# Query product and last group inside TensorE's loop, loads issued from a loop, a transpose in place of three spreads, last values behind w3 and w4

## The chip, the core and the metric

The kernel runs on one core of one Trainium2 chip. The core has five engines that run at the same time and meet through semaphores: TensorE (PE, matrix products), VectorE (DVE), ScalarE (ACT), GpSimd (POOL) and SyncE (SP, which here only issues transfers). Transfers between the chip's main memory (HBM) and the core's own memory (SBUF, 128 partitions) are carried out by 16 DMA engines. The metric is the device time of one execution in microseconds (us), shorter being better. Beside it stands the span, from the first to the last instruction of the one execution that was profiled.

## What is computed

Two blocks run on the same four rows of `x` (batch 4, one token each, width 512), and their results are added:

```python
xn = layernorm(x)
q = (xn @ wq).reshape(4, 1, 32, 128)             # 32 heads of 128
scores = einsum(q, k_cache) * 128 ** -0.5        # k_cache (4, 32, 4096, 128)
o = einsum(softmax(scores), v_cache)             # v_cache (4, 32, 4096, 128)
A = o.reshape(4, 1, 4096) @ wo                   # wo (4096, 512)
x1 = xn                                          # see below
B = x1 + gelu(layernorm(x1) @ w3) @ w4           # w3 (512, 1792), w4 (1792, 512)
out = x + A + B
```

The second block shifts its hidden rows by one or two tokens before `w2`. With one token per row the shift leaves only zeros, so neither kernel loads `w1` or `w2`. Everything is float32. The two caches are 268 MB each, so nearly all that the kernel does is to read 128 pairs (batch, head) of 2 MB of keys and 2 MB of values, once each.

## The kernel before

**Groups.** The 128 pairs (batch, head) are cut into 32 groups of four. A group's keys are 8.39 MB: each of the 128 partitions gets 64 KB, which is 128 cache rows of one head, and each head has 32 partitions. The values are laid out in the same way. Three slots of 8.39 MB in SBUF take the loads in turn: S1 and S0 take the keys of even and odd groups, S2 takes the values.

**One group.** DVE multiplies the keys in place with the query, spread over the rows (two instructions, L330 and L332, one for each half), sums each row over the 128 elements (L335), which gives the scores, and takes the maximum of each head's partitions (L337 to L340). ACT turns the scores into weights `pw` with their row sums `rs` (L238). TensorE contracts weights and values in 32 products (the helper `contract`), four of which share the array, each in 32 output rows. ACT copies the result out of PSUM (L244), and four products with the selector `sel` and one with `ones` turn it into four columns of outputs and sums (`outputs` of TensorE, L246 on ACT), which go to `OS`.

**The order of the work** is written out by hand. The work of each engine is one block (`@block.sync`, `.gpsimd`, `.tensor`, `.scalar`, `.vector`), and the loops over groups are hardware loops (`Fori`) on TensorE, ACT and DVE. SP's 75 loads are unrolled. SP issues them in one queue, and each waits until its slot is free: `k_free` comes from DVE after L335 of that group, `v_free` from TensorE after `contract`. `take` waits for a semaphore and counts it down again.

**The start.** SP issues `wq` in two halves and the keys of group 0 in two halves (L128, L123). TensorE multiplies `wq` outside its loop (32 products), ACT copies and scales two results (L228), DVE transposes them and copies them to `Q` (L316, L317). Only then, on `d_T`, does SP issue the keys of group 1, since their slot S0 holds the scratch data of the start.

**The end.** The values of group 31 go to S1 once the keys of group 30 are used (L141). `w3` and `w4` go to S2 once the values of group 30 are used (L143, L144). `wo` goes to S0 in six pieces once the keys of group 31 are used (L147, L148). After the loop TensorE spreads the outputs of batches 0 to 2 over the operand `X` of the last product (`spread`, with `lt`, which DVE builds in `normalised`), contracts the last values (`VL`), multiplies `w3`, builds the outputs of the last group, spreads batch 3, and multiplies `w4`. DVE and ACT work out gelu in between (L356 to L363, L263, L268). The last part stands in a critical section of its own (from L365 on): TensorE multiplies `wo` piece by piece as the pieces land. Rows 0 to 23 of each partition's 32 go as products of 512 columns into `y`, which ACT copies to `os` (L384) and TensorE adds to `total` by way of `sel`. The other eight rows go straight into `total`, each in four products of 128 columns (L377). DVE and ACT copy `total` to `res` (L386, L388), and SP and ACT each write one half of the output.

Of the kernel before, what the change touches and what calls it, by code (L numbers as in the profile page):

```python
# [7 lines left out]
F32 = mybir.dt.float32  # L8
# [5 lines left out]
P = 128  # L14
# [6 lines left out]
def decode_block(ctx: ExitStack, tc: tile.TileContext, x, k, v, wq, wo, w3, w4, out):  # L21
# [26 lines left out]
    X = sbuf("X", [P, WC, B])  # L48
# [3 lines left out]
    mask = sbuf("mask", [P, 4])  # L52
# [7 lines left out]
    ot = sbuf("ot", [P, JB, HG])  # L60
    rec = sbuf("rec", [P, JB, HG])
    lt = sbuf("lt", [P, H, 4])

    pv, oz, total, y, pa, pb = (nc.alloc_psum_tensor(f"ps{i}", [P, 512], F32) for i in range(6))
# [7 lines left out]
    PIECES = ((0, 8), (8, 16), (16, 24), (24, 28), (28, 31), (31, 32))  # L72
    CUT = 24
    s_x, s_v, s_vl, s_kh, s_h = (sem(n) for n in ("sx", "sv", "svl", "skh", "sh"))
    s_wq = [sem(f"swq{n}") for n in range(2)]
    s_k = [sem(f"sk{n}") for n in range(2)]
    s_wo = s_k + [s_v, s_x, s_kh, s_h]
    d_self, g_a, c_done, d_T, k_free, v_free = (sem(n) for n in ("dself", "ga", "cd", "dT", "kf", "vf"))
# [3 lines left out]
    vf = v.rearrange("b h s d -> (b h s d)")  # L82
# [9 lines left out]
    q_sb = S0[:, 4 * D:6 * D].rearrange("p (n f) -> p n f", n=2)  # L92
    qT = S0[:, 6 * D:8 * D]
    xp = S0[:, 8 * D:8 * D + 2 * P].rearrange("p (e c i) -> p e c i", e=2, c=NC)
    xnT = S0[:, 9 * D:9 * D + P].rearrange("p (c m) -> p c m", c=NC)
    wq_sb = S2[:, :].rearrange("p (c n) -> p c n", c=NC)
    w3_sb = S2[:, :NC * F].rearrange("p (c f) -> p c f", c=NC)
    w34 = NC * F + NF * D
    w4_sb = S2[:, NC * F:w34].rearrange("p (m n) -> p m n", m=NF)
    hs, gu, gt, gT = (S2[:, w34 + n * FT:w34 + (n + 1) * FT] for n in range(4))  # L100
    V3 = S2[:, :].rearrange("p (c d) -> p c d", c=C)
    VL = S1[:, :].rearrange("p (c d) -> p c d", c=C)
# [10 lines left out]

    with tc.tile_critical(no_gpsimd_drain=True), nc.Block(no_gpsimd_drain=True) as block:

        @block.sync
        def _(e):
            def load_k(g):
                e.dma_start(KS[g % 2][:, :], group(kf, g)).then_inc(s_k[g % 2], 16)

            def load_k_half(g, n, s):
                r = slice(n * ROW // 2, (n + 1) * ROW // 2)
                e.dma_start(KS[g % 2][:, r], group(kf, g)[:, r]).then_inc(s, 16)  # L123

            wq_r = wq.rearrange("(p c) n -> p c n", p=P)
            for n in range(2):
                c = slice(n * NC // 2, (n + 1) * NC // 2)
                e.dma_start(wq_sb[:, c, :], wq_r[:, c, :]).then_inc(s_wq[n], 16)  # L128
# [12 lines left out]
            e.dma_start(S1[:, :], group(vf, NG - 1)).then_inc(s_vl, 16)  # L141
            take(e, v_free)
            e.dma_start(w3_sb, w3.rearrange("(p c) f -> p c f", p=P)).then_inc(s_wq[0], 16)  # L143
            e.dma_start(w4_sb, w4.rearrange("(p m) n -> p m n", p=P)).then_inc(s_wq[1], 16)  # L144
            take(e, k_free)
            wo_r = wo.rearrange("(p c) n -> p c n", p=P)
            for n, (c0, c1) in enumerate(PIECES):  # L147
                e.dma_start(wo_sb[:, c0:c1, :], wo_r[:, c0:c1, :]).then_inc(s_wo[n], 16)  # L148

        @block.gpsimd  # L150
        def _(e):
            e.memset(xs, 0.0).then_inc(g_a, 1)
            e.memset(ident[:, :], 0.0).then_inc(c_done, 1)
            e.memset(rs[:, :], 0.0)
            e.memset(pw[:, :, :], 0.0).then_inc(g_a, 1)
# [3 lines left out]
            take(e, s_kh, 16)  # L159
            e.wait_ge(c_done, 2).then_inc(s_h, NG)  # L160

        @block.tensor
        def _(e):
            def contract(V):
                for g in range(G4):
                    t = g % 4
                    i = mm(e, pv[32 * t:32 * t + 32, :], pw[:, g, :], V[:, 4 * g:4 * g + 4, :], g < 4, g >= G4 - 4)
                return i

            def outputs(done):  # L170
                i = mm(e, oz[:, HG:2 * HG], ones[:, :], rs[:, :], True, True)
                if done is not None:
                    i.then_inc(done, 1)
# [4 lines left out]

            def spread(b):
                take(e, d_p)  # L180
                mm(e, pa[:, 32 * b:32 * b + 32], lt[:, :, :], sel[:, :], True, True).then_inc(p_a, 1)

            e.wait_ge(d_T, 1)
            for c in range(NC):
                if c % (NC // 2) == 0:
                    take(e, s_wq[c // (NC // 2)], 16)
                w = wq_sb[:, c, :].rearrange("p (n j h d) -> p n h j d", n=2, j=JB // 2, h=HG)
                for n in range(2):
                    for h in range(HG):
                        i = mm(e, (pa, pb)[n][32 * h:32 * h + 32, :], xnT[:, c, :], w[:, n, h], c == 0, c == NC - 1)  # L190
                    if c == NC - 1:
                        i.then_inc(p_a, 1)

            with nc.Fori(0, NG - 1, 1, engines=[ET.PE]):
                take(e, s_v, 16)
                take(e, a_p)
                contract(V3).then_inc(p_a, 1)
                outputs(v_free)
            for b in range(B - 1):
                spread(b)  # L200
            take(e, a_p)
            take(e, s_vl, 16)
            contract(VL).then_inc(p_a, 1)
            e.wait_ge(s_wq[0], 16)
            for c in range(NC):
                for t in range(4):
                    i = mm(e, pb[32 * t:32 * t + 32, :FT], x1T[:, c, :], w3_sb[:, c, t * FT:(t + 1) * FT],
                           c == 0, c == NC - 1)
            i.then_inc(p_a, 1)
            outputs(None)  # L210
            spread(B - 1)
            mm(e, total[:, 0:P], ident[:, :], base[:, :], True, False)
            e.wait_ge(s_wq[1], 16)
            e.wait_ge(d_p, 1)
# [5 lines left out]
        def _(e):  # L220
# [5 lines left out]
            for n in range(2):  # L226
# [197 lines left out]
```

## Time and profile before

| | |
|---|---|
| median of 3 runs | 1305.07 us (1304.78 to 1305.14) |
| the profiled execution, its own time | 1304.94 us |
| its span | 1303.2 us, so that 1.7 us lie outside it |
| busy share of the span: PE, DVE, ACT | 28%, 90%, 8% |
| granted TensorE clock, mean | 0.627 |
| read from HBM, written to it | 561.00 MB, 0.01 MB |

In the profile an engine's busy time is the time in which its instructions run, and the DMA digits are the busy share of the 16 DMA engines in 40 equal slices of the span. In a row of the timeline stand the start, the duration, the engine with the source line, the operation, what it writes and reads, and in brackets how long the engine stood idle before it and what ended that. "SPq" and "ACTq" are the issuing queues of SP and ACT. L70 and L112 are the helpers `take` and `mm`, through which all of the waits and matmuls go. A float32 product is two MATMUL records, so that 32 products read "x64".

### The profile page before, as it was taken

The page shows a single profiled execution, that of the slowest core. Times are in us where ns is not written, and L with a number is a line of the kernel's source. Part 1 is how long each engine was busy: PE and PEld are TensorE (multiplying, and loading weights), DVE is VectorE, ACT ScalarE, POOL GpSimd, SP SyncE. Part 2 cuts the span into 40 slices and gives each one's busy share as a digit, 9 for nine tenths or more (in the row PEclk, how much of TensorE's full clock was granted, in tenths as well). Part 3 has the DMA queues.
Part 4 walks back from the last instruction along what each step waited for, and adds up shares of the span by engine and source line. Part 5 has one row for each costly group of instructions (what it writes and reads, how often), then busy time and mean ns, then how long its engine had stood idle before and what let it go on. Part 6 is the DMA issues. An engine that isn't in the chain of part 4 may idle for free. (4 is left out here: it accounts for less than half of the span.)

```text
span 1303.2 us, 7027 instructions
## 1 busy us (share of the span) xinstructions
PE 364.8 (28%) x2622; PEld 130.6 (10%) x2622; DVE 1169.3 (90%) x343; ACT 98.9 (8%) x335; POOL 2.1 (0%) x9
## 2 busy tenths in 40 slices
PE   2032123333113333213333212333311333321347
PEld 0010001111001111001111000111000111100112
DVE  4999999999999999999999999999999999999971
ACT  1000000000000000000000000000000000000010
POOL 0000000000000000000000000000000000000000
PEclk9565566666566666566666556666556666655669
DMA  9999999999999999999999999999999999999998
GB/s 403 435 447 422 447 420 449 420 447 422 430 437 424 445 422 447 422 447 422 447 420 449 421 447 422 439 428 428 441 422 447 422 445 424 445 424 445 422 429 347
DMA packets 10830, 561.08 MB, mean 431 GB/s; under 512 B 1212, under 2 KB 1220, under 8 KB 1480
## 3 DMA queue, kind: packets, MB, share of 16 engines
q1 hardware_dynamic: 10808, 561.00, 99.6%
q8 instruction: 3, 0.05, 0.0%
q14 instruction: 3, 0.02, 0.0%
q10 hardware_dynamic: 16, 0.01, 0.0%
HBM read 561.00 MB, written 0.01 MB: 430 GB/s over the span
## 5 line engine op out<-in xcount | busy, mean ns | idle before, releaser
L335 DVE TENSOR_REDUCE sc<-slot 128x128 f32<-128x16384 f32 x32 | 551.0, 17220 | 8.2 <-DVEq L70 8.2
L112 PE MATMUL ps<-slot,pw 128*32 128x512 f32 x2048 | 294.9, 740 | 882.2 <-PEq L70 882.2
L330 DVE TENSOR_TENSOR slot<-slot,qb 128x8192 f32<-128x8192 f32 x32 | 278.1, 8692 | 43.6 <-DVEq L70 43.6
L332 DVE TENSOR_TENSOR slot<-slot,qb 128x8192 f32<-128x8192 f32 x32 | 277.9, 8684 | 2.1 <-DVEq L70 2.1
L112 PEld LDWEIGHTS ps<-slot,pw 128*32 128x32 f32 x2048 | 80.7, 133 | 1071.0 <-issue 1070.9
L238 ACT ACTIVATE pw<-sc,st 32x128 f32<-32x128 f32 x128 | 67.3, 525 | 243.0 <-ACTq L70 241.5
L244 ACT COPY os<-ps 128x512 f32<-128x512 f32 x31 | 18.1, 585 | 857.1 <-ACTq L70 857.1
L112 PE MATMUL ps<-sel,os 128*128 128x4 f32 x256 | 32.8, 252 | 17.5 <-PEq L70 17.5
L112 PEld LDWEIGHTS ps<-sel,os 128*128 128x128 f32 x256 | 31.0, 191 | 19.3 <-issue 19.3
L238 ACT ACTIVATION_READ_ACCUMULATOR pw<-sc,st 32x1 f32 x128 | 26.1, 204 | 0.0
L112 PE MATMUL ps<-slot 128*32 128x512 f32 x92 | 14.0, 747 | 18.8 <-PEq L70 17.6
L327 DVE STREAM_TRANSPOSE qb<-qx 128x128 f32<-128x128 f32 x32 | 10.0, 311 | 4.9 <-DVEq L70 0.5
L386 DVE COPY res<-ps 64x128 f32<-64x128 f32 x1 | 0.3, 283 | 15.2 <-PE ps L112 15.2
L337 DVE TENSOR_REDUCE st<-sc 128x1 f32<-128x128 f32 x32 | 9.2, 286 | 4.7
L356 DVE TENSOR_TENSOR slot<-slot 128x448 f32<-128x448 f32 x1 | 0.6, 624 | 13.1 <-DVEq L70 13.1
L112 PE MATMUL ps<-rs,ones 128*128 128x4 f32 x64 | 12.3, 263 | 0.0
L112 PEld LDWEIGHTS ps<-rs,ones 128*128 128x128 f32 x64 | 9.5, 188 | 26.7 <-issue 26.7
L324 DVE COPY qx<-Q 128x128 f32 x32 | 7.3, 227 | 4.9 <-issue 4.6
L339 DVE STREAM_TRANSPOSE mt<-mx 128x32 f32<-128x32 f32 x32 | 6.8, 211 | 4.7
L340 DVE TENSOR_REDUCE st<-mt 128x1 f32<-128x32 f32 x32 | 6.0, 186 | 4.8 <-DVEq L70 1.8
L338 DVE COPY mx<-st 128x32 f32<-128x32 f32 x32 | 5.8, 181 | 4.7
L246 ACT COPY OS<-ps 128x8 f32 x31 | 5.1, 165 | 42.4 <-ACTq L70 42.4
(58 smaller groups left out, 54.2 us busy)
## 6 DMA issues: line engine op xcount, KB each, us to landing
slot<-in_A_wq_dram SPq DMA_DIRECT2D x2, 4096.0 KB, 16.8
slot<-in_A_k_cache_dram SPq DMA_DIRECT2D x2, 4096.0 KB, 35.8
slot<-in_B_w_dram SPq DMA_DIRECT2D x2, 3584.0 KB, 22.7
slot<-in_A_wo_dram SPq DMA_DIRECT2D x3, 2048.0 KB, 30.1
slot<-in_A_wo_dram SPq DMA_DIRECT2D x1, 1024.0 KB
slot<-in_A_wo_dram SPq DMA_DIRECT2D x1, 768.0 KB, 37.9
slot<-in_A_v_cache_dram SPq DMA_DIRECT2D x32, 28.8
slot<-in_A_k_cache_dram SPq DMA_DIRECT2D x31, 42.3
```

Of the source, the lines that this page charges most:

```text
L112: return e.matmul(o, l, r, start=start, stop=stop)
L238: i = e.activation(o, sc[r, :].rearrange("p (g w) -> p g w", w=4), AF.Exp, bias=st[r, 1:2], scale=1.0, accum_out=rs[r, h:h + 1])
L244: e.copy(os[:, :, :], pv[:, :].rearrange("p (m d) -> p m d", m=4)).then_inc(a_p, 1)
L324: own(e.tensor_copy(qx[:, :].rearrange("p (h r) -> p h r", h=4), Q[:, bass.ds(g + n, 1), :].rearrange("p o h -> p (o h)").unsqueeze(2) .to ...
L327: own(e.transpose(qb[:, :], qx[:, :]))
L330: e.tensor_tensor(out=K[:, :C // 2, :], in0=K[:, :C // 2, :], in1=qw, op=ALU.mult).then_inc(d_self, 1)
L332: e.tensor_tensor(out=K[:, C // 2:, :], in0=K[:, C // 2:, :], in1=qw, op=ALU.mult).then_inc(d_self, 1)
L335: e.reduce_sum(sc[:, :], K, axis=AX.X).then_inc(d_self, 1)
L337: own(e.reduce_max(st[:, 0:1], sc[:, :], axis=AX.X), 2)
L338: own(e.tensor_copy(mx[:, :], st[:, 0:1].to_broadcast([P, 32])))
L339: own(e.transpose(mt[:, :], mx[:, :]))
L340: e.tensor_reduce(st[:, 1:2], mt[:, :], axis=AX.X, op=ALU.max, negate=True).then_inc(d_a, 1)
```

## The change

The edits, in the order of the program:

- The four heads of a group no longer follow each other in memory. Heads 4t + e of one half of a batch (t from 0 to 3, half n of 16 heads) form group (n, e). A load therefore starts at four places in HBM that are 8.39 MB apart, with 32 rows of 64 KB from each. Its source pattern counts 4, 32 and 16384 elements, where it counted 128 and 16384. Its destination still has 128 partitions.
- SP issues the loads of keys and values from a hardware loop over half batches, with addresses from a register. Group 0's keys are one load. `wq` goes in pieces of 20 and 12 products' columns.
- TensorE's loop has 33 turns. Turn 0 multiplies `wq`, with the normalised rows in columns 16 to 23 of `pw`. Turns 1 to 32 contract the values, and the last of them is preceded by the product with `w3` inside a branch. The last 12 products of a turn wait for `v_rest`, which POOL raises 32 times after `wq` and once after the last values.
- ACT has the last group in its loop too, with gelu's copy and tanh in a branch.
- DVE multiplies the keys of a group in one instruction. Its waits on itself count up and are cleared every second group. An alignment directive stands ahead of its program.
- `normalised` runs for 24 groups and then for 8. A 32x32 transpose writes `X` directly, so that `lt`, `mask` and the four spreads are gone. `wo` is read in the order that this asks for, with a source pattern that counts 4, 32 and the row.
- At the end `w3` and `w4` go to S1 after the keys of group 30, and the last values follow them into S2, in two pieces. `wo` still comes last, in pieces of 12, 8, 5, 3, 3 and 1 rows. 28 rows now go into `y`, and the products of `os` and `sel` stand ahead of the last piece.

```diff
-    PIECES = ((0, 8), (8, 16), (16, 24), (24, 28), (28, 31), (31, 32))
-    CUT = 24
+    PIECES = ((0, 12), (12, 20), (20, 25), (25, 28), (28, 31), (31, 32))
+    CUT = 28
+    GF = 20
...
-    kf = k.rearrange("b h s d -> (b h s d)")
-    def group(flat, g):
-        n = HG * S * DH
-        return flat[g * n:(g + 1) * n].rearrange("(p r) -> p r", p=P)
+    kf = k.rearrange("b (n t e) s d -> (b n) e t (s d)", n=2, t=HG).rearrange("m e t (p r) -> m e t p r", p=32)
...
+    nc.vector.addr_align(128, offset=100, max_nops=0)
...
-            load_k_half(0, 0, s_k[0])
-            load_k_half(0, 1, s_kh)
-            e.wait_ge(d_T, 2)
-            load_k(1)
-            for g in range(NG - 1):
-                if g > 0:
-                    take(e, v_free)
-                e.dma_start(S2[:, :], group(vf, g)).then_inc(s_v, 16)
-                if g + 2 < NG:
-                    take(e, k_free)
-                    load_k(g + 2)
-            take(e, k_free)
-            e.dma_start(S1[:, :], group(vf, NG - 1)).then_inc(s_vl, 16)
-            take(e, v_free)
-            e.dma_start(w3_sb, w3.rearrange("(p c) f -> p c f", p=P)).then_inc(s_wq[0], 16)
-            e.dma_start(w4_sb, w4.rearrange("(p m) n -> p m n", p=P)).then_inc(s_wq[1], 16)
+            load_k(0, 0)
+            e.wait_ge(d_T, 1)
+            load_k(0, 1)
+            with nc.Fori(0, NB, 1, engines=[ET.SP]) as m:
+                for i in range(3):
+                    load_v(m, i)
                     take(e, k_free)
+                    if i < 2:
+                        load_k(m, i + 2)
+                e.br_lt(m, NB - 1, on_true="sp_more", on_false="sp_next")
+                with nc.body("sp_more", valid_engines=[ET.SP]):
...
+                    load_k(after, 0)
+                    load_v(m, 3)
+                    take(e, k_free)
+                    load_k(after, 1)
...
+            e.dma_start(w3_sb, w3.rearrange("(p c) f -> p c f", p=P)).then_inc(s_w3, 16)
+            e.dma_start(w4_sb, w4.rearrange("(p m) n -> p m n", p=P)).then_inc(s_w4, 16)
+            take(e, v_free)
+            last = src(vf, NB - 1, 3)
+            e.dma_start(S2[:, FIRST], last[:, :, FIRST]).then_inc(s_v, 16)
+            e.dma_start(S2[:, REST], last[:, :, REST]).then_inc(s_q, 16)
             take(e, k_free)
-            wo_r = wo.rearrange("(p c) n -> p c n", p=P)
+            wo_r = wo.rearrange("(h q c) n -> q h (c n)", h=H, q=4)
...
+            with nc.Fori(0, NG + 1, 1, engines=pe) as g:
+                e.br_lt(g, NG, on_true="pe_turn", on_false="pe_mlp")
...
+                take(e, s_v, 16)
+                take(e, a_p)
+                for n in range(G4):
+                    if n == GF:
+                        take(e, v_rest)
+                    t = n % 4
+                    i = mm(e, pv[32 * t:32 * t + 32, :], pw[:, n, :], V[:, 4 * n:4 * n + 4, :], n < 4, n >= G4 - 4)
+                i.then_inc(p_a, 1)
+                mm(e, oz[:, HG:2 * HG], ones[:, :], rs[:, :], True, True).then_inc(v_free, 1)
...
-                    e.tensor_tensor(out=K[:, :C // 2, :], in0=K[:, :C // 2, :], in1=qw, op=ALU.mult).then_inc(d_self, 1)
-                    take(e, s_h)
-                    e.tensor_tensor(out=K[:, C // 2:, :], in0=K[:, C // 2:, :], in1=qw, op=ALU.mult).then_inc(d_self, 1)
-                    take(e, d_self, 2)
+                    own(e.tensor_tensor(out=K, in0=K, in1=qb[:, :].unsqueeze(1).to_broadcast([P, C, DH]), op=ALU.mult))
...
+                return e.transpose(X[:, b0:b1, :].rearrange("p b h -> p (b h)"), ot[:, b0:b1, :].rearrange("p b h -> p (b h)"))
...
-            if c1 == 28:
+            if n == len(PIECES) - 2:
                 e.wait_ge(a_p, 1)
                 for t in range(4):
-                    mm(e, total[32 * t:32 * t + 32, 0:P], sel[:, :], os[:, (0, 2, 1, 3)[t], :], False, False)
+                    mm(e, total[32 * t:32 * t + B, 0:P], sel[:, 0:B], os[:, (0, 2, 1, 3)[t], :], False, False)
```

Two places of the program show the moved instructions that matter most. The first is DVE's loop over groups, where `qx` and `qb` are the spread query, `slot` the keys and `sc` the scores. Before:

```order
L324 COPY qx<-Q 128x128
L327 STREAM_TRANSPOSE qb<-qx 128x128
L330 TENSOR_TENSOR slot<-slot,qb 128x8192
L332 TENSOR_TENSOR slot<-slot,qb 128x8192
L335 TENSOR_REDUCE sc<-slot 128x128
L337 TENSOR_REDUCE st<-sc 128x1
```

After the change the same place reads:

```order
L318 COPY qx<-Q 128x128
L321 STREAM_TRANSPOSE qb<-qx 128x128
L323 TENSOR_TENSOR slot<-slot,qb 128x16384
L325 TENSOR_REDUCE sc<-slot 128x128
L327 TENSOR_REDUCE st<-sc 128x1
```

The two multiplies are one, and it needs the whole of the group's keys. The second place is the end of TensorE's program, where `X` is the attention's output, `slot` a piece of `wo` (or `w4` in the rows of 32x512), and `os` the copy of `y`. Before:

```order
L112 MATMUL ps<-base,ident 128x128
L112 MATMUL ps<-slot 32x512 x14
L114 UNCONDITIONAL_BRANCH x2
L419 UNCONDITIONAL_BRANCH
L112 MATMUL ps<-slot,X 4x512 x24
L112 MATMUL ps<-slot,X 4x128 x16
L112 MATMUL ps<-os,sel 32x128 x4
L112 MATMUL ps<-slot,X 4x128 x16
```

After the change:

```order
L105 MATMUL ps<-base,ident 128x128
L105 MATMUL ps<-slot 32x512 x14
L108 UNCONDITIONAL_BRANCH x2
L408 UNCONDITIONAL_BRANCH
L105 MATMUL ps<-slot,X 4x512 x28
L105 MATMUL ps<-slot,X 4x128 x12
L105 MATMUL ps<-os,sel 4x128 x4
L105 MATMUL ps<-slot,X 4x128 x4
```

The four products with `os` moved from ahead of the last 16 small products to ahead of the last four.

More of the change, by code (lines that the diff above doesn't have):

```diff
@@ L117, in _ @@
         def _(e):
[L118 to L128, printed above, removed]
@@ L177, in outputs @@
                 i.then_inc(p_a, 1)
[L179 to L211, printed above, removed]
             mm(e, total[:, 0:P], ident[:, :], base[:, :], True, False)
-            e.wait_ge(s_wq[1], 16)
-            e.wait_ge(d_p, 1)
+            e.wait_ge(s_w4, 16)
+            take(e, d_p)
             for m in range(NF):
@@ L266, in _, with mark, own @@
-            e.copy(OS[:, NG - 1:NG, :], oz[:, 0:2 * HG].unsqueeze(1)).then_inc(a_d, 1)
-            e.wait_ge(d_a, 1)
-            e.activation(gt, gu, AF.Tanh, scale=GELU_A).then_inc(a_d, 1)
-            spread(B - 1)
         @block.vector
         def _(e):
-            def own(i, n=1):
+            done = [0]
+            def mark(i):
                 i.then_inc(d_self, 1)
-                take(e, d_self, n)
+                done[0] += 1
+            def own(i):
+                mark(i)
+                e.wait_ge(d_self, done[0])
@@ L277, in _, with clear, rows @@
+            def clear():
+                take(e, d_self, done[0])
+                done[0] = 0
+            def rows(t):
+                return slice(32 * t, 32 * t + 32)
             e.memset(ones[:, :], 1.0)
```

197 lines of the change are left out of this document (104 added, 93 removed).

## The prediction

> **What bounds the kernel now.** I read the page first, for the busy shares of the engines and of the DMA engines.
>
> ```profile
> DMA  9999999999999999999999999999999999999998
> ...
> q1 hardware_dynamic: 10808, 561.00, 99.6%
> ...
> HBM read 561.00 MB, written 0.01 MB: 430 GB/s over the span
> ...
> L335 DVE TENSOR_REDUCE sc<-slot 128x128 f32<-128x16384 f32 x32 | 551.0, 17220 | 8.2 <-DVEq L70 8.2
> ...
> L330 DVE TENSOR_TENSOR slot<-slot,qb 128x8192 f32<-128x8192 f32 x32 | 278.1, 8692 | 43.6 <-DVEq L70 43.6
> L332 DVE TENSOR_TENSOR slot<-slot,qb 128x8192 f32<-128x8192 f32 x32 | 277.9, 8684 | 2.1 <-DVEq L70 2.1
> ```
>
> The 16 DMA engines are busy in every slice, and SP's queue alone fills 99.6% of them. DVE is the next busiest engine, and before L330 it still waits 43.6 us in all, on the keys. Next I read the chain that ended last, in order of time.
>
> ```profile
> 1260.93 37.92 DMA slot<-in_A_wo_dram
> 1298.85 0.04 issue
> 1298.89 1.10 PE ps L112 x32
> ...
> 1300.02 0.28 DVE res L386
> ```
>
> The end waits for the last transfer, which had been queued for 37.92 us behind others. After it comes a tail of 1303.2 - 1298.85 = 4.35 us. The stages at the start show when the transfers began.
>
> ```profile
> 0.00:2.00 2.00, 0.00 (x0) 0.00 (x0) 0.18 (x2) 0.00 (x0) 1.26 (x8) 1.00 0.06 16
> 2.00:4.00 2.00, 0.00 (x0) 0.00 (x0) 0.56 (x2) 0.00 (x0) 0.83 (x2) 1.00 1.03 328
> ```
>
> Data flows from 2.0 us on, 1.0 us after the first issue at 0.96 (quoted below). From there to 1298.85, 561.00 MB make 432.6 GB/s, with no slice that shows a gap. A load of 8.39 MB thus takes about 19.4 us, and a group's two loads 38.7 us. DVE's row means make a group 17.22 + 8.69 + 8.68 = 34.6 us plus small steps. **The kernel is 2.0 us of start, 1296.9 us of transfers and 4.35 us of tail.** The bytes don't change, so a gain must come out of the 6.3 us around the transfers, and a loss must come from a gap, a slower rate or a longer tail.
>
> **The change part by part.** *The start* can leave a gap. These are rows of the timeline.
>
> ```profile
> 0.96 0.87 SPq L128 DMA_DIRECT2D slot<-in_A_wq_dram  x2
> ...
> 17.60 9.01 PE L112 MATMUL ps<-slot 128*32 128x512 f32 x64 [17.60 <-PEq L70]
> ...
> 28.89 0.27 DVE L317 COPY Q<-slot 128x128 f32<-128x128 f32 x1
> 29.18 0.33 SPq L119 DMA_DIRECT2D slot<-in_A_k_cache_dram  x1
> ...
> 32.69 8.69 DVE L330 TENSOR_TENSOR slot<-slot,qb 128x8192 f32<-128x8192 f32 x1 [2.32 <-DVEq L70]
> 43.51 8.69 DVE L332 TENSOR_TENSOR slot<-slot,qb 128x8192 f32<-128x8192 f32 x1 [2.13 <-DVEq L70]
> 52.46 17.22 DVE L335 TENSOR_REDUCE sc<-slot 128x128 f32<-128x16384 f32 x1 [0.26 <-DVEq L70]
> ...
> 69.84 0.33 SPq L119 DMA_DIRECT2D slot<-in_A_k_cache_dram  x1
> ...
> 73.22 0.20 ACT L238 ACTIVATION_READ_ACCUMULATOR pw<-sc,st 32x1 f32 x1
> ...
> 82.22 8.17 PE L112 MATMUL ps<-slot,pw 128*32 128x512 f32 x56 [55.61 <-PEq L70]
> ...
> 106.94 0.33 SPq L119 DMA_DIRECT2D slot<-in_A_k_cache_dram  x1
> ```
>
> The first half of group 0's keys was multiplied at 32.69, the second from 43.51, when it had landed. As one load the keys land at 43.5, and the one multiplication takes 8.69 + 8.68 = 17.4 us, to 60.9 (before: 52.2). With 0.26 us ahead of the sum and 17.22 us for it, `k_free` comes at 78.4, where it came at 69.7, and group 2's keys are issued at 78.5, not 69.84. First data follows 1.0 us later, at 79.5, or up to 0.5 us later still for a register address, an estimate from the 0.33 us that an issue takes. Until then the queue holds `wq`, K0, K1 and V0. By the mean rate they are through at 2.0 + 4 x 19.4 = 79.6; by TensorE, which began on V0 at 82.22, the slowest engine is through somewhat before that. The gap is thus 79.5 to 80.0 against 79.6 to 82.2: between nothing and 0.4 us. I take 0, because the engine that finishes last sets every landing. Next is V1, which waits for the products on V0. The weights of group 0 move by the same 8.7 us, from 73.4 to 82.1, and V0 landed at 82.2, so V1's issue stays. From there on DVE, whose keys are in SBUF already, takes 37.1 us a group (106.94 - 69.84) and gains 1.6 us on the transfers in each, until it waits for keys again.
>
> `Q` is the other thing at the start. The product with `wq` moves into the loop, with 12 products behind its last piece instead of 16, and one copy on ACT and one shorter transpose instead of two copies and a long one. DVE gets two copies into `pw` and a memset. I put `Q` at 28 to 30 us, from 29.16. It costs nothing: K1's issue needs to come only before K0 is through, by the rate at 40.8, and the 11 us between cover it. If they didn't, each us later would be a us of gap.
>
> *The loop on SP.* Issues from registers may take longer than 0.33 us; they are hidden as long as a load waits in the queue.
>
> ```profile
> slot<-in_A_v_cache_dram SPq DMA_DIRECT2D x32, 28.8
> slot<-in_A_k_cache_dram SPq DMA_DIRECT2D x31, 42.3
> ```
>
> Values land 28.8 us after their issue, of which 19.4 are their own transfer: 9 us of cover. Cost 0.
>
> *The rows of a load* are as many and as long as before (128 of 64 KB), from four places instead of one. The trace has only contiguous groups, at 433 GB/s, and I keep that rate. [...]
>
> *The end.*
>
> ```profile
> 1220.42 0.33 SPq L141 DMA_DIRECT2D slot<-in_A_v_cache_dram  x1
> ...
> 1252.67 0.33 SPq L143 DMA_DIRECT2D slot<-in_B_w_dram  x1
> ...
> 1259.13 2.70 SPq L148 DMA_DIRECT2D slot<-in_A_wo_dram  x6
> ...
> 1284.96 4.96 PE L112 MATMUL ps<-slot 128*32 128x512 f32 x28 [1.19 <-DVE slot L363]
> ...
> 1291.06 5.37 PE L112 MATMUL ps<-slot,X 128*4 128x512 f32 x48 [1.13 <-SPq L365]
> ...
> 1296.50 0.58 ACT L384 COPY os<-ps 128x512 f32<-128x512 f32 x1 [12.69 <-PE ps L112]
> ...
> 1297.01 1.06 PE L112 MATMUL ps<-slot,X 128*4 128x128 f32 x32 [0.58 <-DMA slot<-in_A_wo_dram]
> ...
> 1297.89 0.40 PE L112 MATMUL ps<-os,sel 128*32 128x128 f32 x8
> ...
> 1298.89 1.06 PE L112 MATMUL ps<-slot,X 128*4 128x128 f32 x32 [0.60 <-DMA slot<-in_A_wo_dram]
> ```
>
> The same three releases come at the same times, with other loads behind them: `w3` and `w4` (7.34 MB, 17.0 us) at 1220.42, the last values at 1252.67, `wo` at 1259.13. Counted back from 1298.85 at 19.4 us a load, the last values are through at 1279.5, `w3` and `w4` at 1260.1 and the values of group 30 at 1243.1. Each is issued before the one ahead of it is through, the last values by the least, 1260.1 - 1252.67 = 7.4 us. No gap.
>
> TensorE now has the last values late. Their last piece is there at about 1280 to 1281; 12 products take 12/28 of the 8.17 us at 82.22, 3.5 us, and the copy and the four selector products 2 us (an estimate), to about 1286, where the products with `w4` started at 1284.96. With their 4.96 us, and 1.13 us to the last section, `wo` starts at about 1292 instead of 1291.06. 28 products at 5.37/24 = 0.22 us are 6.3 us, to 1298.4 at the latest; `X` and gelu come from DVE behind TensorE's products and are ready by then. Before, 16 small products and the copy of `y` stood behind the 24; now three of the 28 wait for the piece that lands at about 1297, and the copy (0.58 us) ends at about 1298.5 to 1299.2. Behind the piece of 28 to 31 then stand 12 + 4 products, four of them with `os`, and the last four. In before 16 products, 32 records, took 1.06 us, so 20 take 1.33 us. The tail grows by 0.27 us. Its bounds are 0 (the four are done before the last piece lands) and about 1.0 us (`os` late as well).
>
> *The rest* (DVE's counted waits, alignment, transposes for spreads, branches) lies on engines that wait for transfers: 0.
>
> The sum: 1304.94 of the profiled execution + 0.3 = 1305.2. That execution lies 0.13 us below the median of the runs, 1305.07, so the median to expect is **1305.4 us**.
>
> **The rivals.** *Four DMA engines instead of 16* (slower). The new source patterns count 4 in their outermost place. If that count decides over how many engines a load is spread, each load of keys, values and `wo` runs on four of the 16. The trace has transfers of four rows, on ACT's queue.
>
> ```profile
> q10 hardware_dynamic: 16, 0.01, 0.0%
> ...
> slot<-in_A_x_dram ACTq DMA_DIRECT2D x1, 8.0 KB
> ...
> out_dram<-res ACTq DMA_DIRECT2D x1, 4.0 KB
> ```
>
> Two transfers of four rows leave 16 packets: eight rows, and eight more, four each, as if four engines each reported their end. That speaks for it. Against it stands that both sides of those transfers have only four rows, while the new loads still fill 128 partitions from 128 rows; no row shows such a pair. The price: 65 loads of 8.39 MB (32 of keys, 32 of values, `wo`) at 4 x 19.4 = 77.6 us are 5,044 us, with `wq`, `w3` and `w4`, start and tail about 5,090 us. It decides from the first load of keys on. [...] Chance 0.17.
>
> *A real gap before group 2's keys, or a rate a little lower from four places* (slower). If K0's landing, its long multiplication or the issue come 4 us later than worked out, data comes at 84, and some 3 us of gap stay for good: about 1308 us. It decides beyond 2.6 us of gap, since 0.2% is 2.6 us, about what a measurement of this kernel can tell from no change. For it: the margin is the smallest in the program. Against it: every step is a row. A rate 0.5% lower would cost 6.5 us, 1312. Chance 0.06.
>
> *A gain* by over 0.2%. All of the time outside the transfers that could shrink is the 4.35 us tail and the 2.0 us start, and neither loses a step. A better case is the tail's lower bound, 1305.1, or some tenths below. Chance of over 0.2%: 0.02.
>
> **How the numbers follow.** No change by the working above: 0.75; four engines 0.17 and gap or rate 0.06, together slower 0.23; faster 0.02. The predicted time is that of no change. The range runs from 1303.8 (nothing lost, and a us of start or tail saved) to 1308.0 (the tail's 1.0 us and a gap of nearly 2 us), which leaves out the four engines and most of the rest, 0.2 in all.
>
> **What would show it.** Right: DMA digits still at 9 in all slices, landings of values 38.7 us apart, group 2's keys issued near 78.5, products with `wo` starting by 1292 and the last small products ending near 1300.2. A gap shows as TensorE starting on V1 later than about 121 (2.0 + 6 x 19.4, and the 2.6 us by which V0 lay behind that rate). Wrong: DMA digits near 2 and a K load of some 78 us (four engines), a period above 38.8 us (rate), or a span below 1300.

## The result and the profile after

The changed kernel takes 5493.82 us (median of 6 runs, 5460.31 to 5509.85) where the kernel before takes 1304.96 us (1304.78 to 1305.35): 4.2083 times as long, interval 4.1965 to 4.2201. The forecast was 1305.4 us. The profiled execution took 5509.85 us, with a span of 5507.9 us and a mean granted clock of 0.529.

The page of the changed kernel, in the rows that answer to those of before:

```profile
DMA  3222222222222222222222222222222222222321
GB/s 108 59 63 67 76 88 101 109 109 109 109 109 109 109 109 109 109 109 109 109 109 109 109 109 109 109 109 109 109 109 109 109 109 109 109 109 116 111 67 71
DMA packets 9976, 561.06 MB, mean 102 GB/s; under 512 B 360, under 2 KB 368, under 8 KB 756
...
q1 hardware_dynamic: 9956, 560.99, 25.5%
...
L323 DVE TENSOR_TENSOR slot<-slot,qb 128x16384 f32<-128x16384 f32 x32 | 551.2, 17225 | 4013.2 <-DVEq L69 4013.2
...
L325 DVE TENSOR_REDUCE sc<-slot 128x128 f32<-128x16384 f32 x32 | 551.0, 17220 | 4.2
```

DVE does the same 1102 us of work on the keys, but waits 4013 us for them ahead of L323. The bytes are the same. The DMA digits have gone from 9 to 2, and SP's queue fills 25.5% of the 16 engines: four of them, all of the time. The small packets say the same. Before, there are 1212 under 512 B:

```profile
DMA packets 10830, 561.08 MB, mean 431 GB/s; under 512 B 1212, under 2 KB 1220, under 8 KB 1480
```

That is 75 loads x 16 and three transfers of four rows x 4. After, it is 4 loads of `wq`, `w3` and `w4` x 16, 71 loads of keys, values and `wo` x 4, and 3 x 4, together 360. By these counts a load leaves one small packet for each engine that it uses.

Four engines at 433/4 = 108 GB/s do not explain all of it. A table of the changed kernel by stretches, whose last two columns are the DMA share and GB/s, shows two more losses:

```profile
26.00:275.00 249.00, 2.05 (x18) 1.26 (x10) 37.44 (x13) 4.18 (x11) 0.00 (x0) 0.51 0.25 58
275.00:551.00 276.00, 11.16 (x74) 3.92 (x74) 35.85 (x8) 2.86 (x10) 0.00 (x0) 0.51 0.25 65
551.00:826.00 275.00, 9.71 (x74) 3.65 (x74) 58.91 (x10) 2.85 (x10) 0.00 (x0) 0.52 0.25 82
826.00:1000.00 174.00, 10.80 (x74) 3.82 (x74) 34.81 (x9) 2.85 (x10) 0.00 (x0) 0.52 0.25 102
1000.00:5000.00 4000.00, 275.50 (x1924) 98.81 (x1924) 910.95 (x208) 74.25 (x260) 0.00 (x0) 0.53 0.25 109
5000.00:5200.00 200.00, 10.83 (x74) 3.84 (x74) 62.87 (x10) 2.85 (x10) 0.00 (x0) 0.52 0.38 123
5200.00:5508.00 308.00, 43.14 (x306) 12.90 (x306) 12.08 (x18) 5.62 (x16) 0.00 (x0) 0.56 0.20 68
```

At a steady DMA share of 0.25, the rate starts at 58 GB/s and climbs to 109 in 1000 us. Up to there 58 x 249 + 65 x 276 + 82 x 275 + 102 x 174 make 72.7 MB, for which 109 GB/s needs 667 us instead of 974: 307 us lost. In the last 308 us it is 68 GB/s, or 20.9 MB, for which 109 GB/s needs 192 us: 116 us lost. The rival "Four DMA engines instead of 16" was priced at about 5,090 us, with `w3` and `w4` (the 123 GB/s between) on 16 engines already. With the two losses the sum is 5,513, 5 us above the span; rates rounded to 1 GB/s leave some 20 us of it open.

The slow start in the timeline of the changed kernel:

```profile
28.61 0.27 DVE L309 TENSOR_SCALAR Q<-slot 128x128 f32<-128x128 f32 x1
...
180.66 17.22 DVE L323 TENSOR_TENSOR slot<-slot,qb 128x16384 f32<-128x16384 f32 x1 [150.87 <-DVEq L69]
198.02 17.22 DVE L325 TENSOR_REDUCE sc<-slot 128x128 f32<-128x16384 f32 x1
...
215.53 0.55 SPq L116 DMA_DIRECT2D slot<-in_A_k_cache_dram  x1
```

`Q` is there at 28.61, as forecast, but group 0's keys, which begin behind `wq` at about 21 (2.0 + 19.4), come at 180.66. Some 160 us for 8.39 MB are twice what four engines should need, 77.6. And the chain that ended last holds the end:

```profile
5279.21 79.05 SPq L154
...
5358.30 51.31 SPq L154
...
5410.23 60.89 SPq L154
...
5471.15 32.88 DMA slot<-in_A_wo_dram
```

Three of SP's issues of `wo` took 79, 51 and 61 us, where all six together took 2.70 before. During the first two the four engines were busy all the same (a share of 0.25), but at 81 GB/s. Ahead of them, while the last of the values of group 30 came in, the share had fallen to 0.15:

```profile
5200.00:5280.00 80.00, 11.39 (x90) 4.26 (x94) 6.47 (x5) 1.30 (x5) 0.00 (x0) 0.55 0.15 51
5280.00:5410.00 130.00, 9.04 (x64) 2.25 (x56) 4.55 (x9) 2.71 (x8) 0.00 (x0) 0.55 0.25 81
```

The end thus loses first by engines that stand idle, and then by a lower rate of busy ones. That the long issues cost something of their own is not shown.

So three things were open: why four engines, why four engines start at half their rate and need 1000 us to reach it, and what the rest of the change is worth.

### The profile page after: what moved, and what is told of

Its sections match the earlier page's. It is cut to its first block, busy times and chain, and to the rows that moved or that the text cites. A ratio compares the mean times of both kernels' runs of the same rounds, so it can differ in the third digit from the quotient of the medians.

```text
span 5507.9 us, 6988 instructions
## 1 busy us (share of the span) xinstructions
PE 372.2 (7%) x2600; PEld 130.8 (2%) x2600; DVE 1165.4 (21%) x307; ACT 97.3 (2%) x330; POOL 2.1 (0%) x9
## 3 DMA queue, kind: packets, MB, share of 16 engines
q1 hardware_dynamic: 9956, 560.99, 25.5%
HBM read 561.00 MB, written 0.01 MB: 102 GB/s over the span
## 5 line engine op out<-in xcount | busy, mean ns | idle before, releaser
L323 DVE TENSOR_TENSOR slot<-slot,qb 128x16384 f32<-128x16384 f32 x32 | 551.2, 17225 | 4013.2 <-DVEq L69 4013.2
L105 PE MATMUL ps<-slot,pw 128*32 128x512 f32 x2112 | 308.6, 749 | 5053.0 <-PEq L69 5053.0
L105 PE MATMUL ps<-slot,X 128*4 128x512 f32 (+1 forms) x88 | 11.9, 655 | 60.9 <-SPq L354 53.5
```

The costliest lines, as they stand in the source:

```text
L105: return e.matmul(o, l, r, start=start, stop=stop)
L323: own(e.tensor_tensor(out=K, in0=K, in1=qb[:, :].unsqueeze(1).to_broadcast([P, C, DH]), op=ALU.mult))
```

## The experiments

**First round: the source pattern, the places or the loop.** Theory A: the outermost count of the patterns decides over the number of engines. B: four places 8.39 MB apart are slow to read in HBM, whatever engines do it; at half the rate, as the changed kernel begins (58 of 108 GB/s), that would be twice 1,300 us. C: the loop's loads (registers as addresses, patterns of three levels) are slow.

*Rows outside, places inside.* The changed kernel, with the same four places read in another order:

```diff
-.rearrange("m e t (p r) -> m e t p r", p=32)
+.rearrange("m e t (p r) -> m e p t r", p=32)
```

> The changed kernel with one edit: the source patterns of keys, values and wo count 32 (or 32 heads) in the outermost place and 4 inside it, where they counted 4 outside and 32 inside. Addresses, bytes, rows of 64 KB, loop and registers stay; the rows arrive in other partitions, so that the output is not the reference's. Theory A (the outermost count decides over the number of DMA engines): 32 and 128 have 16 as a common divisor, all 16 engines work, and the run takes 1305.4 us, 0.3 us over the kernel before, as the sum of the prediction had it. Rival B (four places 8.39 MB apart in HBM are slow to read whatever engines do it): 2,600 us or more. Rival C (the loop with register addresses, or three-level patterns, make loads slow): near the changed kernel's 5,494 us.

Measured: 1306.16 us (1305.08 to 1307.68) against 1304.98, ratio 1.0009 (1.0000 to 1.0019). From its page:

```profile
DMA  9999999999999999999999999999999999999998
...
DMA packets 10828, 561.06 MB, mean 430 GB/s; under 512 B 1212, under 2 KB 1220, under 8 KB 1608
...
q1 hardware_dynamic: 10808, 561.00, 99.5%
```

The loop, the registers, the three levels and the four places are all still there, and 16 engines run at 430 GB/s. Only the order of the counts changed, and with it the partition in which each row arrives. A stands for the number of engines; B and C fall as causes of the factor.

*Four places without the loop.* The kernel before, unrolled, with `group` returning a pattern of 4 x 32 rows:

```diff
-        return flat[g * n:(g + 1) * n].rearrange("(p r) -> p r", p=P)
+        return flat[g // 4, g % 4]          # [4 places][32 rows][row]
```

> The kernel before with one edit: the source patterns of its unrolled loads of keys and values take four heads 8.39 MB apart, counting 4, 32 and the row, as the changed kernel does; no loop and no register. The heads are paired with other queries, so that the output is not the reference's. wq, w3, w4 and wo stay at 128 rows. Theory A: four engines, DMA share near 25%, 64 loads at 77.5 us or more, 5,000 to 5,500 us. Rival C (loop and registers): 1305 us. Rival B: as A, but with more than four engines busy.

Measured: 5305.34 us. From its page:

```profile
GB/s 117 67 70 75 86 100 109 109 108 109 109 109 109 108 109 109 108 109 109 109 109 108 109 109 108 108 109 109 109 108 108 109 108 108 109 109 109 108 120 125
DMA packets 10050, 561.08 MB, mean 106 GB/s; under 512 B 432, under 2 KB 440, under 8 KB 700
```

432 is 10 loads of weights x 16 + 65 x 4 + 12: four engines again, and the same slow start, without a loop. Where `wo` goes over 16 engines, as here, the end loses nothing (120 and 125 GB/s in the last slices), although SP's six issues of it take 94.44 us in all.

*Eight places of 16 rows* in the same kernel:

```diff
-    kf = k.rearrange("b h s d -> (b h s d)")
+    kf = k.rearrange("b (n t) (e s) d -> (b n) e t (s d)", t=8, e=2).rearrange("m e t (p r) -> m e t p r", p=16)
-        return flat[g * n:(g + 1) * n].rearrange("(p r) -> p r", p=P)
+        return flat[g // 2, g % 2]          # [8 places][16 rows][row]
```

> The kernel before with one edit: the loads of keys and values take eight half heads 2.1 MB apart, so that the source counts 8, 16 and the row. The output is not the reference's. Theory A: eight engines, DMA share near 50%, 64 loads at 38.7 us, with the other loads on 16 engines 2,530 us, more if the eight get in each other's way as the four do in the first 1,000 us of the changed kernel. Rival B: a time that goes with the places, not with the count, so no simple half of the time with four. Rival C: 1305 us.

Measured: 5166.64 us. From its page:

```profile
DMA  5545445454444555454545454545445455445455
GB/s 158 108 108 110 110 110 112 111 113 108 106 104 104 105 106 106 103 106 105 106 104 106 104 105 105 106 103 106 104 105 105 104 105 106 105 107 109 108 109 147
...
q1 hardware_dynamic: 10288, 560.99, 50.3%
```

Eight engines are busy, as the count says, and move no more than four; the time is about twice what A gave for them, 64 x 38.8 us and the rest. 50.3% of 16 x 5164.9 us over 561.00 MB / 65,536 B = 8,560 rows is 4.86 us of an engine for a row of 64 KB. Before it is 99.6% of 16 x 1303.2 us over 8,560, 2.43 us. The count explains which engines work, not how fast.

*One load per head*: the changed kernel, in which each load is four loads of 32 partitions, contiguous in HBM.

```diff
-e.dma_start(KS[i % 2][:, :], src(kf, m, i)).then_inc(s_k[i % 2], 16)
+for t in range(4):
+    e.dma_start(KS[i % 2][32 * t:32 * t + 32, :], src(kf, m, i, t)).then_inc(s_k[i % 2], 16)
```

> The changed kernel with its loads cut by head: each load of 128 rows is four loads of 32 partitions and 32 rows, one for each head, and wq and wo likewise, so that every pattern counts 32 in its outermost place; the waits count 64 instead of 16. It computes the reference. Theory A: 16 engines for each, 1305 to 1308 us, unless 32 partitions at a time are slower to write than 128, for which no run so far has a row. Rival B: 2,600 us or more. Rival C: 5,494 us or more, with four times the issues.

Measured: 2694.12 us (2691.66 to 2699.54), ratio 2.0646 (2.0614 to 2.0677). From its page:

```profile
DMA  9999999999999999999999999999999999999998
...
q1 hardware_dynamic: 14312, 561.01, 100.0%
```

All 16 engines are busy throughout, and every row takes 16 x 2694.3 / 8,560 = 5.04 us, twice its time, though each load reads 2 MB in one piece. There is a second cause, and since each of the four transfers of a load is contiguous in HBM, it does not lie in a source pattern of several places.

**Second round: the partitions written, or HBM.** Theory P, an assumption of the author's: engines that write certain partitions at the same time share one way into SBUF (a port, as one expectation has it). No record shows such a way; what the runs can show is the rate, by the partitions that are written at the same time. So far a load per head, which writes 32 neighbours, takes 5.04 us a row, and in the changed kernel, where each place of a load fills 32 partitions, the four engines begin at 58 GB/s instead of 108. Rival H: the doubled row is HBM's, from places a power of two apart (8,388,608 bytes).

*An odd distance*: as the static kernel with four places, which now lie 127 rows and 21,760 bytes apart.

```diff
+    APART = 127 * ROW + 5440                    # floats; the places were 128 * ROW apart
+        four = flat[n:n + 4 * APART].rearrange("(t a) -> t a", t=4)
+        return four[:, at:at + 32 * ROW].rearrange("t (p r) -> t p r", p=32)
```

> As the kernel before, unrolled and static, with source patterns that count four places of 32 rows, but the places lie 127 rows and 21,760 bytes apart (8,344,832 bytes) in place of 8,388,608, so no power of two is left in the distance; the rows of neighbouring groups overlap, so it reads other rows of K and V than the reference does (as many bytes). Theory P (four DMA engines by the outermost count; two pairs of them write partitions 0 to 31 with 32 to 63 and 64 to 95 with 96 to 127, whose writes share ways into SBUF, and each pair gets half its rate until the two have drifted apart): the distance in HBM is nothing, so the same slow start as with the even distance, 60 to 70 GB/s from 26 to 275 us and 109 from 1000 us, and about 5,300 us (5,240 to 5,360). Rival H (the slow start is HBM's: four places a power of two apart fall on the same part of the memory): 108 GB/s from the first K load, so 64 loads x 77.6 us = 4,966 + 52 for the weights + 6 = about 5,025 us.

Measured: 5302.07 us, 3 us from the even distance, with the same climb (from its page):

```profile
GB/s 116 66 69 75 88 101 109 108 108 109 109 109 109 109 107 108 109 109 109 109 108 108 109 109 109 109 109 107 108 109 109 109 109 108 108 109 109 109 120 126
```

H falls: the distance in HBM does nothing here, one run each.

*Another order of partitions*: the even distance again, but each load is eight transfers of 16 partitions, so that the four engines, in step, write four neighbouring groups of four partitions.

```diff
+        for a in range(8):
+            e.dma_start(to[16 * a:16 * a + 16, :], flat[g // 4, g % 4][:, 4 * a:4 * a + 4]).then_inc(s, 16)
```

> As the static kernel with four places a power of two (8.39 MB) apart, but each K and V load is eight transfers of 16 partitions, each with a source pattern of 4 places x 4 rows, so that the engine of place t writes partitions 16a + 4t to 16a + 4t + 3 for a = 0 to 7: the four engines never write the same group of 4 partitions, nor two groups 32 apart, while they run in step. The rows land in other partitions than the reference needs, so the output is not the reference's. Theory P: four engines, 64 KB packets of 2.42 us from the first K load on, no slow start, 108 GB/s from 26 us: about 5,025 us (4,980 to 5,080). Rival H (HBM): the same distance in HBM, so the same slow start as the run with one transfer a load, 60 to 70 GB/s until 275 us and about 5,300 us. Rival: the slow start is of starting itself (a queue that warms up): 5,300 us too.

Measured: 5045.28 us. From its page:

```profile
GB/s 156 110 108 108 109 108 108 110 108 108 109 108 108 110 108 108 109 108 108 110 108 109 108 108 108 110 108 109 108 108 108 110 108 109 108 108 108 110 118 161
DMA packets 11714, 561.12 MB, mean 111 GB/s; under 512 B 2220, under 2 KB 2228, under 8 KB 2488
```

2220 is 160 + 64 x 8 x 4 + 12: still four engines, from the same four places, and no slow start; 260 us less. The places in HBM and the number of engines are the same in both runs. What differs is what the engines write at the same time, and the number of transfers; 63 more of these cost 5 us in the control below, so the former is taken to decide over the slow start. In one transfer per load the first engine should write partitions 0 to 31 and the second 32 to 63, the third and the fourth likewise, though no record tells which engine writes where. By P the first two share a way, and so do the last two. Two pairs at half rate are 54 GB/s, half of 108, and the table of the changed kernel begins at 58.

*The packets.* The kept traces hold start, time and size of every packet, and each engine ends its part of a load with one of 4 bytes. In the changed kernel the four engines end group 0's keys within 13.3 us of each other, at 166.5 to 179.8 us. Load by load they come further apart. At 994 us they end 0, 9.5, 51.1 and 60.7 us after the first, and so they stay for the next 4000 us: two pairs, with about 9.5 us, four rows, inside each. Up to there this distance grows by a little over 1 us with each load. The median time of a 64 KB packet falls meanwhile from 4.96 us (25 to 100 us) by 2.76 (600 to 700) to 2.42 (1000 to 5000), which is full rate: it is 2.42 before the change too.

Both static kernels with one transfer per load from four places, at the even and at the odd distance, end with 9.5 us in each pair too. In the other order, the four stay within 1.1 us of each other at 2.42 us a packet. With eight places six of the engines stay within 7 us of each other, and the other two, in the end far behind them, within 8 us of one another; the median there is 4.95 to 5.06 us from 100 us on. So the engines do drift apart in these runs, and a pair is at full rate, 2.42 us a packet, once it is some four rows (9.5 us) out of step.

*Halves by partition, halves by column*: the kernel before, each load of 128 rows cut in two in either way.

```diff
+            def halves(to, src, s):
+                for n in range(2):
+                    p = slice(64 * n, 64 * n + 64)                      # control: r = slice(ROW // 2 * n, ROW // 2 * (n + 1))
+                    e.dma_start(to[p, :], src[p, :]).then_inc(s, 16)    # control: to[:, r], src[:, r]
```

> As the kernel before, contiguous groups, but each K and V load of 128 rows is cut in two by partitions, 0 to 63 and 64 to 127, one behind the other on the same queue (the first K load stays in two halves by columns). Computes the reference. Outermost counts are 64, so all 16 engines work, as 16 divides 64. Theory P: each transfer reaches only half of the ways into SBUF, so 64 KB packets of about 5.0 us where before has 2.42: 63 loads x 8 rows an engine x 5.06 us (from the run with a load per head) = 2,550 us, + 19.4 for the first K load + 56 for the weights + 6 = about 2,630 us (2,560 to 2,680), DMA digits 9 and 208 GB/s. The rule of the outermost count alone, and rival H (source contiguous): 1,305 us, at most 1,315 for 63 more transfers.

> Control for the halves by partition: the same cut of each K and V load in two transfers, but by columns, all 128 partitions x 32 KB each. Computes the reference. Theory P, the rule of the outermost count and H alike: 1,305 us (1,304 to 1,310), q1 at 99 to 100%. If it is slower by hundreds of us, the number of transfers costs by itself and the halves by partition show nothing about ports.

Measured: 2636.51 us by partition, 1309.85 by column. From the page of the halves by partition:

```profile
DMA  9999999999999999999999999999999999999998
GB/s 335 207 207 207 208 207 207 207 209 207 207 207 209 207 206 210 212 207 209 207 207 207 207 207 207 207 207 208 207 207 207 208 207 207 207 207 207 207 207 303
```

and from that of the halves by column:

```profile
GB/s 401 432 432 433 433 433 433 432 432 433 432 430 429 430 431 432 433 432 433 433 432 432 433 433 433 430 431 431 430 431 433 432 432 432 433 432 433 433 429 347
```

Contiguous source, outermost counts of 64 and 128, 16 engines busy in both: 64 neighbouring partitions at a time give half the rate, 207 GB/s, and no more than 32 do (208 GB/s with a load per head). The control, with as many transfers of as many bytes, costs 5 us for 63 more transfers than before. P stands in what it says of the rate: the partitions that are written at the same time decide over it here. That shared ways into SBUF are the reason is not shown.

**Third round: what is left of the change at 16 engines**, +1.2 us where the prediction had +0.3. Theory S: the four places cost it. L: the loop's loads or their order.

*The four places without the loop*: the kernel before, with the pattern of the first experiment (32 outside, 4 inside).

```diff
-        return flat[g * n:(g + 1) * n].rearrange("(p r) -> p r", p=P)
+        return flat[g // 4, g % 4]          # [32 rows][4 places][row]
```

> What is left of the change once 16 engines work is 1306.2 against 1305.0, +1.2 us, of which the last copies on ScalarE and the last pieces of wo hold about 0.3; the rest (0.9) is the last landing, with the engines further apart (2.5 us in place of 1.5) from the third K load on. This run: the kernel before, unrolled and static, with the change's four places as source, patterns that count 32 outside and 4 inside; the rows land in other partitions, so the output is not the reference's. Theory S (the four places cost it: neighbouring packets of an engine come from places 8.39 MB apart): 1305.9 us (1305.5 to 1306.4). Rival L (the loop's loads cost it, by issues of 0.54 us with addresses from registers, or the order of the loads around the third K load): 1305.0, within 0.4 of before.

Measured: 1304.84 us (1304.61 to 1305.32) against 1304.94, ratio 1.0000 (0.9991 to 1.0009). S falls, as a cause by itself.

*The loop without the four places*: the changed kernel with contiguous groups and contiguous `wo`.

```diff
-"b (n t e) s d -> (b n) e t (s d)", n=2, t=HG).rearrange("m e t (p r) -> m e t p r", p=32)
+"b (n e t) s d -> (b n) e (t s d)", n=2, t=HG).rearrange("m e (p r) -> m e p r", p=P)
-            wo_r = wo.rearrange("(h q c) n -> q h (c n)", h=H, q=4)
+            wo_r = wo.rearrange("(p c) n -> p (c n)", p=P)
```

> The changed kernel with its loop, its turns and its end, but each group's four heads contiguous as before (128 rows in one piece, outermost count 128) and wo as 128 rows in one piece; heads and wo's rows no longer match, so the output is not the reference's. 16 engines, under 512 B 1212. Theory S (the four places cost the 0.9 us): 1305.3 us, +0.3 for the end alone (1305.0 to 1305.6). Rival L (the loop's loads or their order): 1306.2 (1305.9 to 1306.6), and the engines 2.5 us apart from the third K load on. If both runs lie at +0.5 the two share it.

Measured: 1305.75 us (1305.10 to 1306.67), ratio 1.0007 (0.9998 to 1.0017), between the two. Neither theory holds alone. The traces suggest how they meet. The contiguous loop issues group 2's keys late, as forecast, and TensorE begins on V1 at 121.54:

```profile
78.13 0.34 SPq L116 DMA_DIRECT2D slot<-in_A_k_cache_dram  x1
...
121.54 8.51 PE L105 MATMUL ps<-slot,pw 128*32 128x512 f32 x64 [28.01 <-PEq L69]
```

The static kernel with the four places has a longer issue, but early:

```profile
69.60 0.54 SPq L118 DMA_DIRECT2D slot<-in_A_k_cache_dram  x1
...
121.23 3.96 PE L111 MATMUL ps<-slot,pw 128*32 128x512 f32 x20 [27.82 <-PEq L70]
```

With both, in the changed kernel with rows outside, it is 122.42:

```profile
78.16 0.54 SPq L116 DMA_DIRECT2D slot<-in_A_k_cache_dram  x1
...
82.12 8.63 PE L105 MATMUL ps<-slot,pw 128*32 128x512 f32 x64 [53.38 <-PEq L69]
...
122.42 8.10 PE L105 MATMUL ps<-slot,pw 128*32 128x512 f32 x56 [29.77 <-PEq L69]
```

Before, it began there at 121.36:

```profile
121.36 9.07 PE L112 MATMUL ps<-slot,pw 128*32 128x512 f32 x56 [28.21 <-PEq L70]
```

A late issue that also takes longer leaves a gap of about 1.1 us; one of the two alone leaves -0.1 to 0.2. That is one trace each, and the difference of the medians is within the intervals, so the gap is likely and not shown.

## Why the prediction was wrong

**The step that failed** is "*The rows of a load* are as many and as long as before ... at 433 GB/s, and I keep that rate". The rows are, but the rate is that of as many engines as the outermost counts of both patterns allow, and the source now counts 4. Four engines were a rival with a chance of 0.17, and the profile had the row for it: 16 small packets on q10 for two transfers of four rows. The argument against it, that the load still fills 128 partitions, was no row of the profile but a hope that the longer side decides. The first experiment shows it: with 32 and 128 as outermost counts it is 16 engines and 1306 us, with 4 and 128 four engines and 5494. Eight places gave eight engines, 50.3% of the 16. With a row of the profile for it and none against it, this rival should have been the likeliest case.

**The rival's price**, about 5,090 us, took four engines at full rate. It missed 307 us of slow start and 116 us at the end. The start is put down to the partitions by experiment: the same four engines, in an order in which they should not write partitions 32 apart at the same time, took 260 us less. In the order of the change the rate climbs by itself over some 1000 us, while the packets show the engines of a pair coming 9.5 us apart, and from there it is 109 GB/s, 77 us a load, which is the price's 77.6. With eight places no pair came so far apart and all stayed slow; why these do not drift further stays open. The end fits the same account and was not tried by itself: engines up to 60.7 us apart run dry at different times, which is the share of 0.15, and when they start together again they are slow, the 81 GB/s. What held SP's issues of `wo` stays open.

**The distance in HBM** has no part in this kernel: with the odd distance the time is 3 us from the 5305 of the even one, and 16 engines read the same four places at 430 GB/s. Which partitions are written at the same time was not weighed at all. Halves by partition ran at 207 GB/s and a load per head at 208, against 432 for halves by column, and the run with eight places, at 4.95 to 5.06 us a packet, fits the same account without having been tried further. No run shows the ways into SBUF of which theory P speaks; what the runs show in their place are these rates.

**The rest of the prediction** can be read in the changed kernel with rows outside, where 16 engines run. These are rows of the end of its timeline:

```profile
1290.98 4.48 PE L105 MATMUL ps<-slot,X 128*4 128x512 f32 x40 [1.13 <-SPq L354]
...
1299.31 0.59 ACT L373 COPY os<-ps 128x512 f32<-128x512 f32 x1 [12.98 <-PE ps L105]
1300.07 0.84 PE L105 MATMUL ps<-slot,X 128*4 128x128 f32 x24 [0.82 <-DMA slot<-in_A_wo_dram]
1300.73 0.40 PE L105 MATMUL ps<-os,sel 128*4 128x128 f32 x8
1300.95 0.40 PE L105 MATMUL ps<-slot,X 128*4 128x128 f32 x8
1301.41 0.28 DVE L375 COPY res<-ps 64x128 f32<-64x128 f32 x1 [14.07 <-PE ps L105]
```

- Group 2's keys were forecast to be issued at 78.5: 78.16. TensorE's start on V0, forecast unmoved at 82.22: 82.12. `Q` forecast at 28 to 30: 28.61 in the changed kernel itself.
- The gap there was put at nothing to 0.4 us, and 0 was taken. By TensorE's start on V1 it is 1.1 us (122.42 - 121.36). The allowance for the first data, 0.5 us, came from the time of a short issue.
- `wo` was to start at about 1292: 1290.98. The copy `os` was to end at 1298.5 to 1299.2: 1299.90, of which 1.2 us is the later landing. The last 20 products were to take 1.33 us: from 1300.07 to DVE's copy at 1301.41 it is 1.34, where before it is 1300.02 - 1298.89 = 1.13.
- The sum was +0.3 us; it is +1.2, interval 0 to 2.5, inside the range that was given for this case. The rest of the change thus gains nothing: DVE saves an instruction a group, but it had only waited for keys.

No run beat the kernel before. With 16 engines busy at 99.6% there was nothing to gain but the 6.3 us around the transfers.

## What to carry to other kernels

A load's access pattern set its rate here in two ways, and both can be read before it runs. Take the outermost count of each side: the smaller of the two, and at most 16, was the number of engines in every run here (4 and 128 gave 25.5% of the 16 engines, 8 and 128 gave 50.3%, 32 and 128 gave 99.5%, 64 on both sides 99.9%; all are powers of two, so that a common divisor fits as well). So put the long count outside and split heads inside (which puts the rows into other partitions, so that the rest of the kernel has to follow). Then ask which partitions are written at the same time: transfers on partitions 0 to 63 and 64 to 127 in turn, or on 32 neighbours, ran at half rate with all engines busy (207 and 208 GB/s, against 432). In the profile the first showed as low DMA digits (2 with four engines) and few small packets per load (4 instead of 16), and the second only as a low GB/s at full digits (9).

## What was not expected of the hardware

- Neighbouring partitions, 64 at a time, gave half the rate: 207 GB/s, and 208 for 32, against 432 for 128 cut by columns, all with DMA digits of 9.
- Four engines that began in step took about 5 us for a row of 64 KB and moved 58 to 67 GB/s. Within 1000 us they had drifted 9.5 us apart in pairs, and then took 2.42 us and moved 109 GB/s. Eight stayed near 5 us and at 103 to 113 GB/s.
- The issue of a load with four places took 0.53 to 0.59 us on SP where nothing held it up, in the loop and unrolled alike; a contiguous one took 0.33 to 0.34 in both, once 0.43. So here the pattern sets it, not the register.
- A single issue on SP took up to 79 us at the changed kernel's end, where those of `wo` before took 0.33 to 0.43. In the other order, at 109 GB/s, eight issues took 73 us, so that a low rate is not needed for it.
